# Copying three inputs inside DRAM first, so that the blocks of a VectorE transpose are read and written in order

## The chip, the cores and the metric

The kernel runs on one core of one Trainium2 chip. The metric is the device time of one execution in microseconds, the median of several runs. TensorE (PE in the profile) multiplies matrices, VectorE (DVE) and ScalarE (ACT) work on elements, GpSimd (POOL) helps, and SyncE (SP) issues every DMA of this kernel on one queue.

## What is computed

The reference is a gated linear attention followed by a feed-forward block with the hardswish activation, all in float32.

```
batch, n_heads, seq, head_dim = (4, 8, 768, 48)
for t in range(S):
    state = alpha[:, :, t, :, None] * state + np.einsum('bhd,bhe->bhde', k[:, :, t], v[:, :, t])
    y[:, :, t] = np.einsum('bhd,bhde->bhe', q[:, :, t], state)
x = y.transpose(0, 2, 1, 3).reshape(B * S, H * D)       # 3072 x 384
h = x @ w_in                                            # 384 x 2048
g = h * np.clip(h + 3.0, 0.0, 6.0) / 6.0
out = g @ w_out                                         # 2048 x 384
```

## The kernel before

**Chunks.** The 4 x 768 tokens are cut into 24 chunks of 128 tokens, numbered j = 0 to 23. For a chunk, alpha, k and q are wanted with the feature on the partition (head pair p in 0 to 3; two heads of a pair at partitions 0 and 64) and the token along the free axis. Decay products along the tokens are scans on VectorE (`decay`, L309; `growth`, L320); k and q are scaled by them (`scaled`, L332); scores, masking, the state's update and the output are small matmuls with VectorE and ScalarE work between (`scores` L346, `masked` L356, `update` L429, `attend` L455). Two chunks make a group g; its 256 tokens go through the feed-forward block. From group 2 on, both large products are done by fast matrix multiplication, with sums made on VectorE (L537 to L541, L647, L664) and products on TensorE (`product1`, L600; `product`, L703).

**How a chunk arrives.** `load_akq` (L248) loads alpha, k or q of one chunk. Chunks 0 to 5 are turned on TensorE. From chunk 6 on, a load fills a tile of `quads` (two buffers per name, by j modulo 2, L237) with four DMAs, one per group of 32 partitions (L262): partition u of a group holds tokens 4u to 4u+3, each with its 48 features, so that every run in DRAM is four tokens long (768 bytes, or 640 where the first 32 features are skipped). `by_blocks` (L285) then turns all of it on VectorE in one instruction, 32 x 32 words at a time; since token 4u+v lies at place v of partition u, the output goes to every fourth word ("(u v)" read as "v u"). It serves alpha (`place_alpha`), k and q (`transposed`).

**k by token.** `update` also needs k with the token on the partition. From chunk 8 on, `turn_k` (L388) transposes it back in blocks on VectorE into the k tile of `quads`, `write_k` (L393) writes that to a DRAM tile called far with four DMAs (L396), and `read_k` (L400) reads it back as kb with four more (L404). All wait on the same SP queue as the loads, the loads of v (L272) and the stores of the output (L724).

**The order.** Nothing is scheduled by the compiler: the body ends with one list of words (L751 to L900), and each engine runs its instructions in the order of that list. "la", "lk", "lq" load alpha, k, q; "ca", "tk", "tq" turn them; "kt", "kw", "kr" are the three steps of the exchange through far; "u" the update; "lv" loads v; "O" stores. An engine that waits holds up everything behind it on its own queue only.

The loads and the turn, as they stand:

```
        t = src.rearrange("(p a) (u v) d -> a u p (v d)", a=2, v=V)
        for o in range(4):
            skip = BLK * (o % 2)
            nc.sync.dma_start(out=to[BLK * o : BLK * (o + 1), :, 0 : V * D - skip],
                              in_=t[o // 2, :, :, skip : V * D])
...
        nc.vector.transpose(out=to.rearrange("r p (u v) -> r p v u", v=V),
                            in_=quads[name, j % NQ][:, :, :, 0:BLK])
```

Of the kernel before, what the change touches and what calls it, by code (L numbers as in the profile page):

```python
# [8 lines left out]
FP = mybir.dt.float32  # L9
# [8 lines left out]
def kernel(  # L18
# [32 lines left out]
    nc = tc.nc  # L51
    B, H, S, D = q.shape
# [195 lines left out]
    def load_akq(name, j):  # L248
        src = rows({"a": alpha, "k": k, "q": q}[name], j)
        if j < FIRST:  # L250
            nc.sync.dma_start(out=ring[name, j % NR][:, :, 0:D],
                              in_=src.rearrange("h s d -> s h d"))
            return
        to = quads[name, j % NQ]
        if j < FIRST + NQ:
            for o in (BLK, 3 * BLK):
                nc.gpsimd.memset(to[o : o + BLK, :, V - 1, D - BLK : BLK], 1.0)
        to = to.rearrange("r p v d -> r p (v d)")
        t = src.rearrange("(p a) (u v) d -> a u p (v d)", a=2, v=V)
        for o in range(4):  # L260
            skip = BLK * (o % 2)
            nc.sync.dma_start(out=to[BLK * o : BLK * (o + 1), :, 0 : V * D - skip],  # L262
                              in_=t[o // 2, :, :, skip : V * D])

# [20 lines left out]
    def by_blocks(to, name, j):  # L285
        nc.vector.transpose(out=to.rearrange("r p (u v) -> r p v u", v=V),
                            in_=quads[name, j % NQ][:, :, :, 0:BLK])
# [433 lines left out]
    def store2(g, i):  # L721
# [8 lines left out]
        "lq": lambda j: load_akq("q", j), "lv": load_v, "w": load_weight,  # L730
# [19 lines left out]
    with tc.manual_schedule():  # L750
# [3 lines left out]
               dx.0 w.2 d2.2 kb.1.0 ck.1 lq.1 r.2 sm.0.1 st.1 tq.1.2 q.1 d3.2 z.0.3 d1.2 dx.2 lv.1.1  # L754
               u.1.3.1 sv.1.0 sm.1.0 p.2 sm.1.1 sc.1.0.2 m.1 ya.0.3 yb.0 cy.0 lq.2 w.1 d1.1 tq.2.1
               q.2 d4.2 lk.2 tk.2.3 k.2 fa.2.0 d4.0 st.2 sc.2.0.2 d2.1 d3.1 m.2 dx.1 d4.1 qa.1.1
               lk.3 la.3 ta.3.1 ca.3 la.4 fa.0.1 sv.1.1 w.3 r.3 ta.4.3 ca.4 r.4 tk.3.1 k.3 kb.2.0
               qa.1.0 d2.3 ya.1.2 yb.1 cy.1 fa.1.2 lq.3 ck.2 d1.3 p.3 d3.3 lv.2.2 u.2.3.2 sm.2.0
               d4.3 fb.2 tq.3.1 q.3 fb.1 qa.2.0 sm.2.1 sv.2.0 st.3 fr.0.2.0 fg.0.2 lk.4 tk.4.0
               sv.2.1 w.5 d2.5 k.4 d3.5 d1.5 qa.3.0 d4.5 qa.2.1 sc.3.1.3 m.3 w.6 d2.6 d1.6 d3.6 d4.6  # L760
               lv.3.0 lq.4 w.7 kb.3.2 fb.0 f.0.3.3 kb.4.0 ya.2.1 ck.3 u.3.3.2 sm.3.0 fr.0.3.1 fg.0.3
               fr.0.1.0 fg.0.1 qa.3.1 sv.3.0 sm.3.1 p.4 d2.7 sv.3.1 d1.7 d3.7 d4.7 f.0.5.0 fr.0.5.1
               fr.0.0.0 fg.0.5 fg.0.0 tq.4.3 ck.4 la.5 ta.5.2 f.0.6.3 ca.5 w.4 d2.4 ya.3.0 yb.3 cy.3
               fr.0.6.1 yb.2 cy.2 w.9 d2.9 q.4 qa.4.1 d1.4 d1.9 dx.4 la.6 w.8 d3.4 r.5 lk.5 w.10
               d3.9 p.5 ca.6 fg.0.6 d4.9 w.12 lq.5 lv.4.1 d2.8 d3.8 f.0.7.2 d1.8 st.4 d4.8 d4.4 w.11
               fr.0.7.0 fg.0.7 f.1.7.0 fr.1.7.1 fg.1.7 sc.4.0.2 m.4 f.1.1.1 fr.1.1.0 fg.1.1 f.1.3.3
               fr.1.3.1 d2.10 d1.10 tk.5.3 f.1.0.2 d2.12 d3.10 d4.10 w.13 fg.1.3 fr.1.0.0 fg.1.0 k.5
               d3.12 lq.6 f.1.6.0 f.1.2.1 u.4.1.0 sm.4.0 d1.12 d4.12 sv.4.0 qa.4.0 ya.4.2 fr.1.6.1
               fg.1.6 w.15 tq.5.3 fa.4.3 sv.4.1 d2.11 kb.5.1 d2.13 fr.1.2.0 f.1.4.2 fr.1.4.1 d1.11
               sm.4.1 q.5 r.6 d3.11 d3.13 fg.1.4 d4.11 lv.5.0 lk.6 tq.6 p.6 d2.15 d3.15 fg.1.2 d1.13  # L770
               d4.13 sc.5.0.3 yb.4 f.1.5.0 fr.1.5.1 fg.1.5 tk.6 m.5 b.1.0.2 fb.4 b.1.1 d1.15 d4.15
               st.5 y.5 w.14 la.7 lk.7 cy.4 d2.14 qa.5.1 ck.5 b.0.0.1 fr.0.4.0 d3.14 k.6 q.6 ca.7
               fg.0.4 d1.14 d4.14 x.0 y.1 y.10 b.0.1 y.0 y.2 u.5.2 P.1.0.0 K.1.0 qa.5.0 sv.5.0
               qa.6.1 P.1.1.3 b.0.2 b.1.2 kb.6.0 ya.5.3 y.6 s.1.0.0 sm.5.0 sv.5.1 G.1.0.0 tk.7
               s.1.1.1 s.1.2.3 x.1 yb.5 cy.5 b.1.3 sc.6.1.2 lv.6.2 ck.6 u.6.3.0 s.1.3.2 x.2 P.1.2
               b.0.3 K.1.1 y.7 s.1.4 s.1.5 y.11 y.3 r.7 xc.2.1 x.3 y.4 y.8 xc.2.3 k.7 xc.2.0 xc.2.4
               y.9 y.12 y.16 y.13 y.15 P.1.3.3 K.1.2 P.1.4 bo.1 P.1.5 xc.2.5 G.1.1.1 P.1.6 y.14 y.17
               y.19 xc.2.6 sm.6.0 G.1.2.2 y.20 M.2.0.2 lv.12.1 la.8 O.1.1 O.1.0 ca.8 y.18 y.21 y.23
               so.1 G.1.3.3 n.2.0.8 bo.0 lq.7 lv.7.0 O.1.2 m.6 xc.2.2 xc.2.10 xc.2.7 tq.7 r.8 p.7
               xc.2.8 sv.6.1 M.2.15.3 M.2.1 kb.7.3 n.2.1.9 M.2.16 M.2.2 n.2.2.10 M.2.7.0 n.2.7.11  # L780
               sm.6.1 xc.2.9 q.7 p.8 M.2.3 M.2.4 n.2.4.12 M.2.8 o.2.0.0 M.2.5 n.2.5.13 qa.7.0 sv.6.0
               st.7 lk.8 O.1.3 lq.8 lk.9 la.9 la.10 tk.8 tq.8 lq.10 lq.9 ya.6.1 yb.6 M.2.9 z.1.3
               M.2.18.1 o.2.1.0 e.2.1.1 M.2.10 cy.6 ck.7 sc.7.0.2 u.7.1.3 n.2.10.14 M.2.11 qa.7.1
               ca.9 la.11 y.22 M.2.6.2 h.2.1 q.8 m.7 e.2.0.0 h.2.0 n.2.11.15 qa.6.0 n.2.18.10 qa.8.1
               M.2.12 M.2.19 n.2.12.12 M.2.13 sm.7.0 sv.7.1 r.9 k.8 o.2.3.0 sv.7.0 ya.7.0 y.24
               o.2.5.0 n.2.13.12 o.2.2.0 yb.7 cy.7 sc.8.1.2 xc.3.1 o.2.2.1 e.2.2.1 xc.3.3 o.2.3.1
               M.2.14 xc.3.4 xc.3.0 xc.3.5 o.2.4.0 xc.3.7 xc.3.6 o.2.6.0 P.2.0.1 M.3.0.2 M.2.17
               h.2.2 o.2.6.1 e.2.3.0 h.2.3 o.2.7.0 K.2.0 n.3.0.12 M.3.1 n.3.1.9 e.2.5.1 M.3.7.0
               n.3.7.13 xc.3.8 o.2.7.1 xc.3.2 kt.8 e.2.6.0 h.2.6 tk.9 M.3.2 n.3.2.10 e.2.4.0 P.2.1.3
               h.2.4 h.2.5 s.2.0.14 e.2.7.0 G.2.0.1 h.2.7 M.3.3 M.3.4 n.3.4.8 k.9 s.2.1.11 M.3.8  # L790
               o.3.0.0 ca.10 kt.9 P.2.3.3 s.2.2.15 s.2.3.14 lv.8.2 kw.8 kr.8 lk.10 sm.7.1 xc.3.9
               M.3.5 n.3.5.11 K.2.2 e.3.0.1 xc.3.10 M.3.9 o.3.1.0 P.2.2 K.2.1 u.8.0.3 M.3.18.2 s.2.5
               M.3.10 n.3.10.14 n.3.18.15 e.3.1.0 s.2.4 P.2.4 tq.9 h.3.0 st.8 sv.8.0 M.3.11 n.3.11.8
               tk.10 p.9 sm.8.0 q.9 r.10 k.10 qa.9.0 qa.9.1 m.8 sm.8.1 h.3.1 M.3.19 o.3.5.0 kt.10
               P.2.5 G.2.2.0 st.9 M.3.12 sc.9.0.1 qa.8.0 n.3.12.10 o.3.3.0 kw.9 lv.9.0 kr.9 sv.8.1
               u.9.2.3 sm.9.0 sv.9.1 sv.9.0 G.2.1.2 sm.9.1 st.10 M.3.15.2 M.3.16 M.3.6.3 M.3.13 m.9
               o.3.4.0 o.3.6.0 tq.10 n.3.13.10 o.3.2.0 e.3.4.1 ya.8.2 yb.8 ya.9.3 yb.9 cy.9 M.3.14
               M.3.17 cy.8 xc.4.1 P.2.6 e.3.5.0 G.2.3.3 o.3.2.1 xc.4.3 h.3.4 xc.4.4 o.3.6.1 xc.4.5
               xc.4.0 xc.4.6 e.3.2.1 M.4.0.0 n.4.0.10 P.3.0.1 xc.4.7 o.3.7.0 p.10 h.3.5 o.3.3.1
               xc.4.8 M.4.7.3 M.4.1 xc.4.2 h.3.2 o.3.7.1 lk.11 O.2.2 tk.11 e.3.6.0 e.3.3.1 h.3.3  # L800
               P.3.1.2 e.3.7.1 n.4.1.13 M.4.2 K.3.0 ca.11 q.10 h.3.6 r.11 k.11 h.3.7 n.4.7.15
               lv.10.2 lv.11.0 kw.10 sc.10.0.1 kr.10 G.3.0.0 u.10.3.2 sm.10.0 qa.10.1 n.4.2.14 M.4.3
               M.4.4 M.4.8 s.3.0.9 xc.4.9 s.3.2.12 s.3.1.11 P.3.3.2 n.4.4.8 M.4.5 o.4.0.0 e.4.0.0
               sv.10.1 sm.10.1 xc.4.10 kt.11 O.2.0 O.2.3 lq.11 m.10 s.3.3.9 s.3.5 M.4.9 o.4.1.0
               P.3.2 sv.10.0 st.11 n.4.5.11 K.3.2 la.13 M.4.18.0 p.11 tq.11 lk.12 tk.12 K.3.1 M.4.10
               n.4.10.9 q.11 qa.10.0 n.4.18.12 e.4.1.1 la.12 s.3.4 ca.12 h.4.0 r.12 P.3.5 G.3.2.1
               h.4.1 M.4.11 P.3.4 n.4.11.8 M.4.12 n.4.12.14 qa.11.0 M.4.19 p.12 G.3.1.3 lq.12 kw.11
               O.2.1 tq.12 kr.11 u.11.3 sc.11.0.2 sv.11.0 O.3.1 lk.13 P.3.6 qa.11.1 M.4.6.2 G.3.3.2
               k.12 o.4.3.0 m.11 sm.11.0 sv.11.1 kt.12 M.4.13 n.4.13.14 q.12 o.4.3.1 e.4.3.0 o.4.2.0
               o.4.6.0 h.4.3 o.4.2.1 ya.10.1 ya.11.0 yb.10 yb.11 cy.11 cy.10 xc.5.1 ca.13 xc.5.3  # L810
               M.4.15.1 M.4.16 M.4.14 P.4.0.2 o.4.4.0 M.4.17 xc.5.4 o.4.5.0 xc.5.0 xc.5.5 M.5.0.0
               o.4.6.1 e.4.2.1 h.4.2 P.4.1.3 qa.12.1 e.4.4.0 xc.5.6 o.4.7.0 h.4.4 o.4.7.1 tk.13
               K.4.0 n.5.0.14 M.5.1 e.4.7.1 h.4.7 e.4.5.0 xc.5.2 h.4.5 xc.5.7 G.4.0.3 e.4.6.1 h.4.6
# [119 lines left out]
```

## Time and profile before

| | us |
|---|---|
| median of 3 runs (lowest, highest) | 535.48 (535.39, 535.66) |
| span of the profiled execution, first to last instruction | 533.7 |
| TensorE busy in it | 524.6 |
| VectorE busy in it | 477.2 |
| ScalarE busy in it | 257.2 |
| share of the 16 DMA engines taken by the one queue | 42.5% |

The profile records one execution. The span leaves out what lies before the first and after the last instruction; against the median that is 1.8 us. Matmuls are pipelined and their ends are modelled, so a busy TensorE is not by itself a TensorE at its peak; the waits say more. The granted TensorE clock is 1.00 throughout.

### The profile page before, as it was taken

Reading aid. Unit: us, or ns where it says so; the run is one execution under the profiler, and the core shown is the slowest. Engines: PE = TensorE matmul, PEld = TensorE weight load, DVE = VectorE, ACT = ScalarE, POOL = GpSimd, SP = SyncE. Lnnn points to the kernel's source line nnn. Section 1 sums busy time; section 2 is a strip of 40 time slices with the busy share of each in tenths; the row PEclk is TensorE's granted clock in tenths of the full one; section 3 lists DMA queues with packets and bytes.
Section 4 is the critical chain, followed back from the end, with each engine's and each line's share of the span. In section 5 each row is a group of like instructions: output and inputs, shape, how many; then the busy total and the mean of one; then the engine's idle time right before and its main releaser. Section 6 shows DMA issues by size and latency. Waiting matters only on the chain.

```text
span 533.7 us, 15143 instructions
## 1 busy us (share of the span) xinstructions
PE 524.6 (98%) x6306; PEld 499.4 (94%) x6306; DVE 477.2 (89%) x849; ACT 257.2 (48%) x503; POOL 50.4 (9%) x71
## 2 busy tenths in 40 slices
PE   8799999999999999999999999999999999999997
PEld 7698886789999999999999999999999999999997
DVE  6999989999999999998999999999999899496382
ACT  3889865212653553553544444642634544553340
POOL 5333425100000000000000000000000000000000
DMA  9998876005615155254344355044454042100001
GB/s 174 217 252 256 215 216 152 21 2 154 152 30 116 32 121 135 57 140 95 87 110 113 91 124 140 19 120 102 115 136 104 11 110 43 44 2 2 15 16 37
DMA packets 124100, 54.40 MB, mean 102 GB/s; under 512 B 83328, under 2 KB 116864, under 8 KB 124032
## 3 DMA queue, kind: packets, MB, share of 16 engines
q1 hardware_dynamic: 124032, 53.44, 42.5%
q8 instruction: 49, 0.80, 0.6%
q14 instruction: 19, 0.16, 0.1%
HBM read 44.50 MB, written 8.91 MB: 100 GB/s over the span
## 4 chain that ended last, share of the span: by engine, by line
PE 85%; DVE 8%; POOL 2%; DMA 2%; ACT 1%; issue 1%; SPq 1%; DVEq 0%; POOLq 0%
PE m_ps L703 34%; PE m_ps L600 34%; PE m_ps L478 5%; PE t_ps L455 4%; PE t_ps L346 2%; PE t_ps L429 2%; PE m_ps L489 2%; PE t_ps L282 1%; DVE rings L647 1%; DMA v<-in_v_dram 1%; DVE raw L537 1%; ACT raw L191 1%; DMA kq<-in_k_dram 1%; DVE g_sb L647 1%; DVE w L537 1%
## 5 line engine op out<-in xcount | busy, mean ns | idle before, releaser
L606 ACT COPY g_sb<-m_ps 128x512 f32<-128x512 f32 x110 | 63.6, 584 | 124.9 <-PE m_ps L600 104.1
L703 PE MATMUL m_ps<-w,g_sb 128*128 128x192 f32 x704 | 121.7, 327 | 0.0
L703 PEld LDWEIGHTS m_ps<-w,g_sb 128*128 128x128 f32 x704 | 113.7, 190 | 0.4
L703 PE MATMUL m_ps<-rings,g_sb 128*128 128x192 f32 x528 | 91.5, 326 | 0.0
L703 PEld LDWEIGHTS m_ps<-rings,g_sb 128*128 128x128 f32 x528 | 85.4, 190 | 0.1
L600 PE MATMUL m_ps<-xc,w 128*128 128x128 f32 x640 | 82.7, 277 | 0.3 <-DVE w L541 0.3
L600 PEld LDWEIGHTS m_ps<-xc,w 128*128 128x128 f32 x640 | 77.5, 192 | 1.5 <-issue 0.5
L494 ACT ACTIVATE r<-g_sb,half 128x512 f32<-128x512 f32 x80 | 56.8, 722 | 32.9 <-DVE g_sb L541 12.1
L498 DVE SCALAR_TENSOR_TENSOR g_sb<-r,g_sb 128x512 f32<-128x512 f32 x80 | 53.6, 682 | 4.6 <-ACT r L494 4.2
L600 PE MATMUL m_ps<-xT,raw 128*128 128x128 f32 x400 | 52.5, 277 | 0.0
L600 PEld LDWEIGHTS m_ps<-xT,raw 128*128 128x128 f32 x400 | 48.6, 192 | 0.6
L409 POOL TENSOR_TENSOR st<-sm,R 128x192 f32<-128x192 f32 x20 | 12.9, 643 | 353.8 <-DVE sm L439 306.7
L647 DVE TENSOR_TENSOR g_sb<-g_sb 128x512 f32<-128x512 f32 (+1 forms) x55 | 42.0, 795 | 0.2
L600 PE MATMUL m_ps<-xT,w 128*128 128x128 f32 x320 | 42.0, 276 | 0.0
L600 PEld LDWEIGHTS m_ps<-xT,w 128*128 128x128 f32 x320 | 39.3, 192 | 0.1
L366 ACT COPY A<-q 48x256 f32<-48x256 f32 x88 | 35.5, 404 | 5.0 <-DVE q L332 3.7
L356 DVE TENSOR_TENSOR A<-t_ps,mask 64x256 f32<-64x256 f32 x96 | 36.0, 414 | 0.4
L478 PE MATMUL m_ps<-xT,w 128*128 128x256 f32 x144 | 32.8, 382 | 0.0
L600 PE MATMUL m_ps<-xc,raw 128*128 128x128 f32 x240 | 31.8, 276 | 0.0
L309 DVE TENSOR_TENSOR_SCAN R<-t,ones 128x516 f32<-128x516 f32 x24 | 29.7, 1236 | 1.1 <-ACT t L300 1.0
L478 PEld LDWEIGHTS m_ps<-xT,w 128*128 128x128 f32 x144 | 26.7, 190 | 3.6
L600 PEld LDWEIGHTS m_ps<-xc,raw 128*128 128x128 f32 x240 | 29.6, 192 | 0.1
(104 smaller groups left out, 731.0 us busy)
## 6 DMA issues: line engine op xcount, KB each, us to landing
raw<-in_moe_w_out_dram SPq DMA_DIRECT2D x8, 768.0 KB, 5.2
raw<-in_moe_w_in_dram SPq DMA_DIRECT2D x6, 768.0 KB, 6.8
v<-in_v_dram SPq DMA_DIRECT2D x48, 96.0 KB, 3.0
out_dram<-oh SPq DMA_DIRECT2D x44, 96.0 KB, 1.7
far<-kq SPq DMA_DIRECT2D x64, 64.0 KB, 2.2
kb<-far SPq DMA_DIRECT2D x64, 64.0 KB, 2.0
aq<-in_alpha_dram SPq DMA_DIRECT2D x36, 96.0 KB, 2.5
qq<-in_q_dram SPq DMA_DIRECT2D x36, 96.0 KB, 2.4
```

The source lines that it names most:

```text
L309: nc.vector.tensor_tensor_scan(out=reverse(R, n - 1, n), data0=reverse(ax, n, n), data1=reverse(ones, n, n), initial=0.0, op0=ALU.mult, op ...
L356: nc.vector.tensor_tensor(out=to[:, a], in0=sc[a][half], in1=mask[half, half].unsqueeze(1).to_broadcast([HB, NP, HB]), op=ALU.mult)
L366: nc.scalar.copy(out=to[:, a], in_=Q_t[j][64 * a : 64 * a + D, :, half])
L409: nc.gpsimd.tensor_tensor(out=st, in0=sm, in1=R_t[j][:, :, 0:1].to_broadcast([C, NP, D]), op=ALU.mult)
L455: nc.tensor.matmul(y_of(j, (i + 1) // 2, p)[:, HB * b : HB * b + HB], vb[:, p, e : e + 32], A_t[j][:, b, 2 * p + a], start=(b == 0 and i = ...
L478: nc.tensor.matmul(h[:, f], w1[:, kk, o : o + C], xT_t[g][:, kk], start=(kk == 0), stop=(kk == KT - 1))
L494: nc.scalar.activation(out=to, in_=h, func=AF.Relu, bias=half, scale=1.0 / 6.0)
L498: nc.vector.scalar_tensor_tensor(out=to, in0=r, scalar=1.0, in1=h, op0=ALU.min, op1=ALU.mult)
L600: nc.tensor.matmul(acc[g][i][:, f * C : (f + 1) * C], spots[w][:, f * C : (f + 1) * C], x_of(g, x), start=(first and f == 0), stop=last, s ...
L606: nc.scalar.copy(out=slots[z], in_=acc[g][i])
L647: nc.vector.tensor_tensor(out=out, in0=in0, in1=in1, op=ALU.subtract)
L703: nc.tensor.matmul(to[g], a, rhs[:, f], start=(first and f == 0), stop=(last and f == HF - 1), skip_group_check=True)
```

## The change

For chunks 10 to 23 (`MOVED = 10`), a new step `move` ("mv" in the list) copies alpha, k and q of the chunk from the inputs to DRAM tiles ma, mk and mq, which have two buffers each: one DMA per name, eight runs of 6144 words, head order (pair, a) turned into (a, pair). `load_moved` then fills the tile of `quads` from the copy, in another layout: partition u of a group of 32 holds token 32v+u at place v, so that one run is the 32 features (or the last 16) of one token, 128 or 64 bytes; four DMAs per load as before, each with 512 runs. The pads behind the 16 features, which the long runs used to fill with other data, are set once per buffer on GpSimd. `by_blocks` reads the tile and writes its output in order.

```
+        if j >= MOVED:
+            load_moved(name, j)
+            return
...
+    def in_blocks(name, j):
+        t = quads[name, j % NQ].rearrange("r p v d -> r (p v d)")[:, 0 : NP * C]
+        return t.rearrange("r (p v d) -> r p v d", p=NP, v=V)
+
+    def move(j):
+        for name, t in (("a", alpha), ("k", k), ("q", q)):
+            to = moved_t[name, j] = far.tile([2, NP, C * D], FP, tag="m" + name, name="m" + name)
+            nc.sync.dma_start(out=to, in_=rows(t, j).rearrange("(p a) s d -> a p (s d)", a=2))
+
+    def load_moved(name, j):
+        to = in_blocks(name, j)
+        if j < MOVED + NQ:
+            for o in (BLK, 3 * BLK):
+                nc.gpsimd.memset(to[o : o + BLK, :, :, D - BLK : BLK], 1.0 if name == "a" else 0.0)
+        to = to.rearrange("r p v d -> r (p v) d")
+        t = moved_t.pop((name, j)).rearrange("a p (v u d) -> a u (p v) d", u=BLK, v=V)
+        for o in range(4):
+            skip = BLK * (o % 2)
+            n = min(BLK, D - skip)
+            nc.sync.dma_start(out=to[BLK * o : BLK * (o + 1), :, 0:n],
+                              in_=t[o // 2, :, :, skip : skip + n])
...
     def by_blocks(to, name, j):
+        if j >= MOVED:
+            nc.vector.transpose(out=to.rearrange("r p (v u) -> r p v u", v=V),
+                                in_=in_blocks(name, j))
+            return
```

In the list of words only the fourteen "mv" are new; every other word keeps its place. mv.10 and mv.11 stand ahead of la.8. Each later mv.j stands right behind the last load of chunk j-2, whose copies' buffers it takes over:

```
... lv.12.1 mv.10 mv.11 la.8 O.1.1 O.1.0 ca.8 ...
... lv.8.2 kw.8 kr.8 lk.10 mv.12 ... kw.9 lv.9.0 kr.9 ...
... lq.11 mv.13 ... la.13 ... lk.12 ... lq.12 mv.14 kw.11 ... kr.11 ...
... kr.12 la.14 ... lk.14 lq.13 mv.15 O.3.0 O.3.3 lv.13.2 kw.13 O.4.0 lq.14 mv.16 ... lq.15 ...
... lk.20 mv.22 ... kw.19 kr.19 ... lk.21 mv.23 kw.20 ...
```

## The prediction

> **What bounds the kernel now.** I read the page's busy row first, then the chain that ended last, then who waited for whom on TensorE from 110 us on, then the VectorE groups with shapes kept apart, and last the DMA queue: its issues in order of time, and its packets in single windows. The columns of the busy row are busy time, share of the span and instructions; the next row is the chain's share by engine; the last is TensorE's only wait after 110 us (total, times, longest).
>
> ```profile
> PE 524.6 (98%) x6306; PEld 499.4 (94%) x6306; DVE 477.2 (89%) x849; ACT 257.2 (48%) x503; POOL 50.4 (9%) x71
> PE 85%; DVE 8%; POOL 2%; DMA 2%; ACT 1%; issue 1%; SPq 1%; DVEq 0%; POOLq 0%
> PE m_ps L600 <- DVE w L541: 0.3, 1, 0.3
> ```
>
> TensorE carries the end. In the chain, VectorE stands only before 128.04 us; from there to 530.8 us every piece is a matmul, and the one wait is 0.3 us, at 128 us. VectorE is busy 89%, but nobody on TensorE waits for it later. The first operation that the change touches on VectorE is the alpha transpose of chunk 10, at 163.2 us. So whatever VectorE saves there has at most tenths of a us to give.
>
> The two kinds of transpose that matter (line, shapes, count | busy, mean ns | idle before):
>
> ```profile
> L286 DVE STREAM_TRANSPOSE q<-qq 128x512 f32<-128x512 f32 x18 | 20.2, 1121 | 0.0
> L286 DVE STREAM_TRANSPOSE t<-aq 128x512 f32<-128x512 f32 x18 | 20.1, 1115 | 0.0
> L391 DVE STREAM_TRANSPOSE kq<-k 128x512 f32<-128x512 f32 x16 | 11.2, 697 | 0.0
> ```
>
> L286 writes every fourth word, L391 writes runs of 32 words; same size, 1.12 against 0.70 us.
>
> Now the queue that the change loads. The first three rows are SP's issues around chunk 9 (start, time, line, transfer, count); the fourth is the matmuls of that chunk's state update on TensorE.
>
> ```profile
> 163.28 2.23 SPq L262 DMA_DIRECT2D kq<-in_k_dram  x4
> 165.61 2.57 SPq L396 DMA_DIRECT2D far<-kq  x4
> 169.85 1.82 SPq L404 DMA_DIRECT2D kb<-far  x4
> 179.72 0.82 PE L429 MATMUL t_ps<-v,kb 64*64 64x48 f32 x32
> ```
>
> Every chunk from 8 on sends its k through DRAM (far, then kb) on this one queue, and `update` needs kb. The last of the four kb reads is issued three quarters into its row and lands 2.0 us later (the page's median): 173.2 us for chunk 9, 6.5 us ahead of its use at 179.72. The same difference for chunks 9 to 23 is 6.5, 3.5, 4.8, 6.9, 4.5, 6.5, 4.0, 5.9, 9.3, 4.7, 4.2, 5.8, 12.9, 3.3 and 6.7 us, median 5.8. That is all the cover that this exchange has.
>
> Last, what packets cost, in four windows that hold nearly one kind each (packets, MB, share of 16 engines):
>
> ```profile
> q1 hardware_dynamic: 205, 0.63, 46.6%
> q1 hardware_dynamic: 3102, 1.94, 62.5%
> q1 hardware_dynamic: 1161, 0.25, 30.0%
> q1 hardware_dynamic: 1584, 0.20, 41.2%
> ```
>
> 68 to 72 us holds 3 KB packets of w_out: 46.6% of 4 us times 16 engines, over 205, is 145 ns each. 133.3 to 146 holds the present loads (768 and 640 bytes): 40.9 ns. 146 to 150 is mostly v (192 bytes): 16.5 ns. 157 to 160 is the far write (128 bytes): 12.5 ns.
>
> **The change, part by part.** *Transposes.* 42 of them (alpha, k, q of chunks 10 to 23) now write in runs as L391 does: 42 x (1.12 - 0.70) = 17.6 us less on VectorE; the bounds are 0, if the order of the words doesn't matter, and these 17.6. On the path: 0. The only wait that it could shorten is the 0.3 us above, and that lies before them.
>
> *Pads.* Twelve memsets of 32 partitions on GpSimd, at the loads of chunks 10 and 11. They wait for the buffers of chunks 8 and 9; GpSimd is idle for 31.5 us before its work at 166.65 us. 0.
>
> *Loads.* Each has 4 x 512 pieces of 128 or 64 bytes in place of 4 x 128 long ones. Issuing 512 pieces takes SP 0.65 us (far: 2.57 for four), a present load's 0.465: 0.74 us more per load. On the engines 2048 x 16.5 ns / 16 = 2.1 us replaces 512 x 40.9 / 16 = 1.3 us; bounds 1.6 us (12.5 ns) and 5.2 us (40.9 ns). I take 16.5, the nearest row: short pieces from DRAM to SBUF. With room on the queue the extra is hidden; behind the copies it adds the 0.74 us once to each hold-up below.
>
> *Copies.* Three per chunk, DRAM to DRAM, 196,608 bytes each, as eight runs of 24,576. How many of the 16 engines share one, the trace doesn't show: every transfer before has 32, 64 or 128 outermost steps. It shows that runs aren't cut (2,112 packets between 156.7 and 161.0 us, where one far exchange issues four times 512 runs), so at most eight engines can work on eight runs. The source's outermost step counts only 2 (the two heads of a pair, a=2, then four pairs), the destination's 8. Bounds: eight engines with one run each, or two with four runs each. By the w_out row a run is 8 x 145 ns = 1.16 us: 1.2 us a copy on eight, 4.65 us on two. I take two, because whole outermost steps are what both sides can hand out without cutting either; both ends stay in play. [...]
>
> The speed itself has bounds too. The share reads 138.0% between 9 and 14 us, so packets on an engine overlap up to 1.4 deep, and a copy may take 4.65 / 1.38 = 3.4 us. Nothing in the trace reads and writes DRAM at once; if that halves the speed, it is 9.3 us. I take 4.65, the row with the longest packets.
>
> *What is queued behind them.* SP's order is otherwise the same. Each copy set stands right behind the last load of chunk j-2, whose landing it waits for (2.4 us by the page's medians, mostly beside the first copy's own drain). In most places the next transfers are the far/kb exchange of an earlier chunk: after the copies of 12 come far and kb of 9, after 14 those of 11, after 15 of 13, after 17 of 14, after 22 of 19. Those need all 16 engines, the two busy ones also, and come after the three copies there: 3 x 4.65 = 14.0 us. With 0.7 us for a load, less the 5.8 us of cover, TensorE stands still 14.0 + 0.7 - 5.8 = 8.9 us, 12 times (chunks 12 to 23): 107 us. The copies of 10 and 11 go out near 91 us, where SP otherwise waits until 121.67; six of them drain in 28 us, by 119, and the alpha load of chunk 8 behind them lands near 121, ahead of its transpose at 124.83. 0, with 3 us to spare.
>
> *Sum.* The profiled span is 533.7 us; the median of the runs is 535.5, so 1.8 us lie around it. 533.7 + 107 + 1.8 = 642 us.
>
> A cross-check by load alone: per chunk the two engines carry 14.0 (copies) + 6.3 (three loads) + 1.1 (v) + 1.6 (far) + 0.8 (kb, eight packets of 2 KB each at two thirds of 145 ns) + 0.7 (two output stores) = 24.5 us, where TensorE takes 19.7 us per chunk ((464.16 - 168.73) / 15). Even with perfect overlap 14 x 4.8 = 67 us are missing, which would be 603 us.
>
> **Rivals.** *Hidden copies (not slower).* If a copy runs on eight engines, three hold the queue for 3.5 us, under the 5.8 us of cover; then nothing reaches TensorE, VectorE's 17.6 us are off the path, and the time stays 535.5. It decides where a copy takes less than about 1.8 us. For it: the eight runs, and SP's long idle stretches (127 us waiting for outputs alone). Against: the outermost 2, and the least covers of 3.3 and 3.5 us, which such a hold-up could still graze.
>
> *Half speed.* Copies at 9.3 us: 27.9 + 0.7 - 5.8 = 22.8 us, 12 times, 274 us, and 809 us. For it: both ends in DRAM. Against: far's writes into DRAM cost 12.5 ns a packet, less than v's reads from it.
>
> *Small packets dear.* If the 64- and 128-byte reads cost 40.9 ns each, loads take 5.2 us in place of 2.1, 9.3 us more per chunk: 24.5 + 9.3 - 19.7 = 14.1 us, 14 times: 197 us, and 733 us. For it: present loads cost 40.9 ns; against: v's 192-byte pieces cost 16.5.
>
> **How the numbers follow.** A measurement can tell about 0.2%, or 1.1 us, from no change. The forecast, two engines at 3.4 to 7.2 us a copy: 0.80. Hidden copies: 0.11, of which 0.08 within 0.2%, 0.02 faster and 0.01 slower by a grazed cover. Half speed: 0.05; dear packets: 0.04. Faster 0.02, same 0.08, slower 0.90. The range goes from the copy at 3.4 us (12 x (10.2 + 0.7 - 5.8) = 61 us, 597; some covers are longer, so 588) to one at 7.2 us (12 x 16.5 = 198, 734) and the dear packets' 733; up to 740. It leaves out hidden copies, half speed, and little more.
>
> **What would show it.** Right: TensorE's waits led by L429, the update, on the kb transfer; far and kb landing over 10 us after issue where they follow copies; copies landing one after another some 4 to 5 us apart; the transposes at 0.70 us; VectorE's idle time growing by far more than it saves. Wrong: copies landing within 3 us of issue and TensorE still without waits, or TensorE waiting for something other than a transfer behind a copy.

## The result, and the profile after

| | before | after |
|---|---|---|
| median of the runs, us (lowest, highest) | 535.57 (535.39, 535.73) | 631.64 (631.19, 634.57) |
| span of the profiled execution | 533.7 | 629.5 |
| TensorE busy in it | 524.6 | 544.3 |
| VectorE busy in it | 477.2 | 464.0 |
| mean granted TensorE clock | 1.00 | 0.932 |

The changed kernel is slower: ratio 1.181, 95% interval 1.178 to 1.183. The forecast was 642, range 588 to 740.

Lines are shifted by the change: the far write is L428, the kb read L436, the update L461, the copies L278, the moved loads L290. First the busy row and the chain's shares of the page, then TensorE's waits from 110 us on (total, times, longest):

```profile
PE 544.3 (86%) x6306; PEld 517.3 (82%) x6306; DVE 464.0 (74%) x849; ACT 257.6 (41%) x503; POOL 54.1 (9%) x83
PE 50%; DVE 16%; SPq 16%; DMA 12%; issue 2%; POOL 1%; ACT 1%; DVEq 0%; POOLq 0%
PE t_ps L461 <- DMA kb<-far: 56.9, 10, 14.9
PE t_ps L461 <- DMA v<-in_v_dram: 15.5, 1, 15.5
PE m_ps L735 <- DVE g_sb L679: 2.9, 1, 2.9
```

One wait of 0.3 us has become 76 us of waits, nearly all at the update, on transfers. With the 19.7 us that TensorE is busy longer, they make up the 95.8 us by which the span grew. TensorE's share of the chain falls from 85% to 50%, and SP's own sequencer holds 16% where it held 1%.

Each moved transpose got as short as was reckoned (moved layout, then the old one, which chunks 6 to 9 keep):

```profile
L315 DVE STREAM_TRANSPOSE k<-kq 128x512 f32<-128x512 f32 x14 | 9.9, 706 | 5.2 <-DMA kq<-mk 5.2
L318 DVE STREAM_TRANSPOSE k<-kq 128x512 f32<-128x512 f32 x4 | 4.4, 1110 | 0.0
```

Now the same place as before, the exchange of chunk 9. SP's issues in order of time (start, time, line, transfer, count), and then the first matmuls of the update on TensorE, with their wait in brackets:

```profile
166.90 0.66 SPq L278 DMA_DIRECT2D ma<-in_alpha_dram  x1
167.60 0.64 SPq L278 DMA_DIRECT2D mk<-in_k_dram  x1
168.28 0.60 SPq L278 DMA_DIRECT2D mq<-in_q_dram  x1
168.98 9.39 SPq L428 DMA_DIRECT2D far<-kq  x4
...
182.35 1.72 SPq L436 DMA_DIRECT2D kb<-far  x4
```

```profile
184.89 0.42 PE L461 MATMUL t_ps<-v,kb 64*64 64x48 f32 x2 [5.05 <-DMA kb<-far]
```

Three copies go out in 1.9 us. The far write behind them takes SP 9.39 us to issue in place of 2.57: SP doesn't merely see it land late, it is held in the issue itself. kb then leaves 12.5 us later than before (182.35 against 169.85), the cover was 6.5 us, and TensorE waits 5.05 us.

How fast a copy is shows where nothing else runs, in the stretch after the first six copies (110 to 114 us; 40 slices of 0.1 us, GB/s in each; then packets, MB, share of 16 engines):

```profile
GB/s 0 0 0 0 0 0 246 0 246 0 0 0 0 0 0 246 0 246 0 0 0 0 0 0 246 0 246 0 0 0 0 0 0 246 0 0 246 0 0 0
q1 hardware_dynamic: 10, 0.20, 11.4%
```

Each 246 is one packet of 24,576 bytes. They end in pairs, one pair every 0.9 us, and the share is that of two engines (2 of 16 is 12.5%): each of two engines moves a run in 0.91 us, 27 GB/s, and a copy of eight runs takes 3.65 us. Two engines is what the forecast took from the source's outermost step of 2; the trace now agrees. The 3.65 us are nearer to its lower bound, 3.4 us from overlapping packets (4.65 / 1.38), than to the 4.65 us taken from the w_out row.

### The profile page after: what moved, and what is told of

The parts are those of the page before. It is cut to its first block, busy times and chain, and to the rows that moved or that the text cites. A ratio compares the mean times of both kernels' runs of the same rounds, so it can differ in the third digit from the quotient of the medians.

```text
span 629.5 us, 15199 instructions
## 1 busy us (share of the span) xinstructions
PE 544.3 (86%) x6306; PEld 517.3 (82%) x6306; DVE 464.0 (74%) x849; ACT 257.6 (41%) x503; POOL 54.1 (9%) x83
## 4 chain that ended last, share of the span: by engine, by line
PE 50%; DVE 16%; SPq 16%; DMA 12%; issue 2%; POOL 1%; ACT 1%; DVEq 0%; POOLq 0%
PE m_ps L632 17%; PE m_ps L735 17%; SPq L428 6%; DMA far<-kq 6%; SPq L290 5%; PE m_ps L510 5%; PE t_ps L487 3%; PE t_ps L461 2%; DMA mq<-in_q_dram 2%; DMA kb<-far 2%; PE m_ps L521 2%; DVE g_sb L679 2%; SPq L436 2%; DVE g_sb L530 2%; DMA v<-in_v_dram 1%
## 5 line engine op out<-in xcount | busy, mean ns | idle before, releaser
L735 PE MATMUL m_ps<-w,g_sb 128*128 128x192 f32 x704 | 123.6, 330 | 0.0
L735 PEld LDWEIGHTS m_ps<-w,g_sb 128*128 128x128 f32 x704 | 115.7, 193 | 0.5
L735 PE MATMUL m_ps<-rings,g_sb 128*128 128x192 f32 x528 | 95.3, 336 | 2.9 <-DVE g_sb L679 2.9
L735 PEld LDWEIGHTS m_ps<-rings,g_sb 128*128 128x128 f32 x528 | 89.0, 197 | 3.3 <-DVE g_sb L679 3.1
L632 PE MATMUL m_ps<-xc,w 128*128 128x128 f32 x640 | 85.8, 284 | 0.3 <-DVE w L573 0.3
L461 PE MATMUL t_ps<-v,kb 64*64 64x48 f32 x704 | 21.4, 244 | 74.5 <-DMA kb<-far 56.9
L461 PEld LDWEIGHTS t_ps<-v,kb 64*64 64x64 f32 x704 | 18.0, 156 | 78.4 <-issue 62.4
L632 PEld LDWEIGHTS m_ps<-xc,w 128*128 128x128 f32 x640 | 80.7, 198 | 1.5 <-issue 0.4
L530 DVE SCALAR_TENSOR_TENSOR g_sb<-r,g_sb 128x512 f32<-128x512 f32 x80 | 53.6, 683 | 13.4 <-ACT r L526 13.2
L632 PE MATMUL m_ps<-xT,raw 128*128 128x128 f32 x400 | 56.2, 290 | 0.0
L632 PEld LDWEIGHTS m_ps<-xT,raw 128*128 128x128 f32 x400 | 52.2, 204 | 0.7
L441 POOL TENSOR_TENSOR st<-sm,R 128x192 f32<-128x192 f32 x20 | 12.9, 644 | 419.9 <-DVE sm L471 365.0
L471 DVE TENSOR_TENSOR s<-t_ps,st 128x192 f32<-128x192 f32 x20 | 7.0, 352 | 56.7 <-PE t_ps L461 37.7
L632 PE MATMUL m_ps<-xT,w 128*128 128x128 f32 x320 | 42.9, 280 | 0.0
L632 PEld LDWEIGHTS m_ps<-xT,w 128*128 128x128 f32 x320 | 40.1, 195 | 0.1
L632 PE MATMUL m_ps<-xc,raw 128*128 128x128 f32 x240 | 31.8, 276 | 0.0
```

What stands on the lines that cost most here:

```text
L461: nc.tensor.matmul(ps_t["u", j, b][64 * a : 64 * a + 64, p], kb_t[j][half, p, 64 * a : 64 * a + 64], v_t[j][half, b, 2 * p + a, 0:D], star ...
L530: nc.vector.scalar_tensor_tensor(out=to, in0=r, scalar=1.0, in1=h, op0=ALU.min, op1=ALU.mult)
L632: nc.tensor.matmul(acc[g][i][:, f * C : (f + 1) * C], spots[w][:, f * C : (f + 1) * C], x_of(g, x), start=(first and f == 0), stop=last, s ...
L735: nc.tensor.matmul(to[g], a, rhs[:, f], start=(first and f == 0), stop=(last and f == HF - 1), skip_group_check=True)
```

## The experiments

Each was run with the kernel before on the same chip, whose medians were 535.49 to 535.65 us. All intervals are 95%.

**1. The copies alone.** Loads and transposes stay as they were before; the copies are made and nobody reads them.

```
-        if j >= MOVED:
-            load_moved(name, j)
-            return
```

(and the same in `by_blocks`)

> Only the copies of the changed kernel, three per chunk in the same places, and nobody reads them: loads from the inputs in long runs and transposes as before the change. Theory (the copies alone make the hold-ups): TensorE still waits 50 to 80 us for kb and v, and the time is 600 to 632 us. Rival A (short pieces): without them the time is 535 to 545. Rival B (waits for landings between copies and loads): those links are gone here too, so the time falls below 570.

Measured: 620.17 us (619.46 to 621.42), ratio 1.158 (1.157 to 1.160). TensorE's waits:

```profile
PE t_ps L454 <- DMA kb<-far: 47.8, 10, 12.3
PE t_ps L454 <- DMA v<-in_v_dram: 13.6, 1, 13.6
```

The copies by themselves, read by no one, cost 84.7 of the 96.1 us, with the same two waits. The loads with their short pieces add 11.5.

**2. The transposes alone.** Only the order of the words written by the transposes of chunks 10 to 23 is changed, with the loads of before; the tokens of those chunks then stand in another order.

```
-        nc.vector.transpose(out=to.rearrange("r p (u v) -> r p v u", v=V),
-                            in_=quads[name, j % NQ][:, :, :, 0:BLK])
+        to = to.rearrange("r p (v u) -> r p v u" if j >= 10 else "r p (u v) -> r p v u", v=V)
+        nc.vector.transpose(out=to, in_=quads[name, j % NQ][:, :, :, 0:BLK])
```

> The kernel before with one edit: the transposes of chunks 10 to 23 write in runs. The loads are unchanged, so tokens come out in another order; the order is what is left out. Theory: VectorE's busy time falls by about 17 us (42 transposes from 1.12 to 0.70 us), TensorE has no waits to shorten, and the time stays within 0.2% of before, 534.5 to 536.5 us. Rival (VectorE's pace sets TensorE's somewhere that the waits don't show): 525 to 533 us.

Measured: 535.48 us, ratio 1.000 (0.9991 to 1.0009). The busy row against that of before:

```profile
PE 524.4 (98%) x6306; PEld 499.4 (94%) x6306; DVE 463.5 (87%) x849; ACT 257.2 (48%) x503; POOL 50.4 (9%) x71
```

VectorE works 13.7 us less and nobody gains. The whole aim of the change is worth nothing here. That it is 13.7 us and not the 17.6 of 42 shorter records comes from overlap: the next instruction used to start 0.96 us after such a transpose (median) and now starts 0.63 us after it, and 42 x 0.33 = 13.9 us.

**3. More outermost steps per copy.** The copy is cut by head parity into two DMAs, first with four outermost steps (four runs of 24,576 bytes each), then with sixteen (1,536 bytes each).

```
+            src = rows(t, j).rearrange("(p a) (g s) d -> a g p (s d)", a=2, g=16)
+            for a in range(2):
+                nc.sync.dma_start(out=to[a].rearrange("p (g x) -> g p x", g=16), in_=src[a])
```

> The changed kernel with each copy cut in two (one per parity) of four runs of 24,576 bytes, so that four engines share it. Theory: six runs of 0.91 us on each of four engines, 5.5 us a set in place of 10.9; against a median cover of 5.8 us less 0.7 for a load, hold-ups of 0 to 3 us remain at the chunks with the least cover: waits of 2 to 12 us, 537 to 550 us, and clock losses small. Rival A (short pieces): above 575 us. Rival C (the bytes written to and read from DRAM, however spread): as the changed kernel, 620 to 632 us.

> The changed kernel with each copy cut in two transfers (one per parity of the head) of 16 outermost steps of 1,536 bytes, so that 16 engines can share it; loads, transposes and places in the list as in the changed kernel. Theory (two engines hold up the exchange): a set of copies keeps an engine busy for about 0.6 us per name in place of 3.65, TensorE's waits after 128 us fall from 76 us to under 2, the granted clock stays at 1.00, and the time is 535 to 537 us. Rival A (the short pieces of the loads jam the queue): they are all still here, so the waits stay above 30 us and the time above 575. Rival B (SP is held by the landings that the copies wait for and by twice as many copy issues, six of 0.6 us): waits of 10 to 40 us remain, 550 to 580 us.

Measured: four steps 564.12 us, ratio 1.054 (1.052 to 1.055); sixteen steps 549.36 us, ratio 1.027 (1.025 to 1.030). Both are above what the theory allowed, and the second is nearly at its rival B (549.4 us against 550, waits of 9 us against 10), which the next experiment takes up. But the order is as it should be, if a copy runs on as many engines as it has outermost steps. That was the author's assumption; these runs show the times alone: two steps 631.6 us, four 564.1, sixteen 549.4. With sixteen the page gives a copy half 2.4 us to landing, and the waits are small:

```profile
PE t_ps L463 <- DMA kb<-far: 6.2, 5, 2.2
PE t_ps L463 <- DMA v<-in_v_dram: 3.0, 1, 3.0
```

The bytes are the same; 82 of 96 us went with more outermost steps, 67.5 of them already with four, where the runs are as long as before. 13.9 us are left, which "copies on all engines are free" doesn't explain.

**4. Another issuer.** First the sixteen-step copies, then the copies of the change itself, issued by GpSimd on its own queue; nothing else is changed.

```
-                nc.sync.dma_start(
+                nc.gpsimd.dma_start(
```

> As the kernel with copies on sixteen engines (split by head parity, six DMAs per chunk, 549.4 us), but the copies are issued by GpSimd on a queue of its own, at the same places in the list. Theory (what is left of the loss there, 14 us, is SP's time for 84 more issues and its waiting for the buffers of the copies, with far and kb behind them): TensorE's waits shrink from 11.5 us to under 4, and the time is 536 to 540 us. Rival (the moved loads with their 2,048 short pieces, or the traffic of the copies, are what is left): 545 to 552 us. Rival (GpSimd's own work, the state's update, waits behind the copies, or the copies wait behind it): over 555 us, with new waits of TensorE on GpSimd or on loads.

> The changed kernel with its copies as they are (one DMA of eight runs, two engines), issued by GpSimd on its own queue. Theory (SP is held while it issues far behind the copies, 9.4 us for four issues in place of 2.6, and far and kb stand behind the copies in one queue): with two queues the packets of far and kb take turns with the copies' on the two engines, SP is free, and what is left is those engines' load: 11 us of copies plus 10.5 us of other packets per chunk against 19.7 us of TensorE, 14 x 1.8 = 25 us, so about 545 to 570 us. Rival (the two engines finish the copies' 24,576-byte packets first whatever queue they come from, and every transfer waits for its last packet there): 600 us or more. Rival (two queues hide it all): under 540 us.

Measured: sixteen steps 536.22 us, ratio 1.0010 (1.0002 to 1.0019); eight runs 554.63 us, ratio 1.035 (1.033 to 1.037). TensorE's waits, of the first and of the second kernel, and the far write of chunk 9 in the second:

```profile
PE t_ps L463 <- DMA v<-in_v_dram: 0.3, 1, 0.3
PE m_ps L634 <- DVE w L575: 0.2, 1, 0.2
```

```profile
PE t_ps L461 <- DMA kb<-far: 6.2, 2, 5.6
PE t_ps L461 <- DMA v<-in_v_dram: 5.6, 1, 5.6
```

```profile
168.89 4.39 SPq L428 DMA_DIRECT2D far<-kq  x4
```

The first removes the remaining 13.9 us down to 0.6: the moved loads and the traffic, which this kernel still has, are harmless, and what was left of the loss came with the copies' place on SP's queue (84 issues more, and what stood behind them).

The second is the surprise: the change's copies, on another queue, cost 19 us in place of 96. The range of its theory is met, but not by its mechanism, two engines shared by two queues. The runs are still whole: both pages count 404 packets of 8 KB or more, the copies' 336 among them (the rest of GpSimd's 3,360 packets are under 512 bytes). But the copies ran on more engines at once. The first six move 148 GB/s from 96 to 100 us and take 50.6% of the time of the 16 engines, with nothing else on them; on SP's queue it was 49 GB/s and 11.4%. They also leave at other times, since GpSimd doesn't stand in SP's line (the set ahead of chunk 9's far write at 163.50 us in place of 166.90). So how much of the 77 us is the queue and how much the engines stays open.

In the first kernel the change of issuer was worth 13 us; the 77 us of the second don't measure it, since the engines changed too.

**5. Doses.** The kernel before, with 1, 2, 3, 4 and 6 unread copies put right ahead of the far write of five chunks.

```
+    def copies(j, n):
+        for i in range(n):
+            to = far.tile([2, NP, C * D], FP, tag=f"m{i}", name=f"m{i}")
+            nc.sync.dma_start(out=to, in_=rows((alpha, k, q)[i % 3], j).rearrange(
+                "(p a) s d -> a p (s d)", a=2))
```

> The kernel before, with copies that nobody reads (one DMA of eight runs of 24,576 bytes each, as in the change) put right before the far write of five chunks: 1 copy before that of chunk 10, 2 before 13, 3 before 15, 4 before 18, 6 before 20. All loads, layouts and transposes are those of before. Theory (a copy holds the queue for 3.65 us, two engines at 912 ns per packet, and a wait is the sum of the copies less the cover): covers of 3.5, 4.5, 4.0, 4.7 and 5.8 us give waits of TensorE at the five updates of about 0 to 1, 2.8, 7, 9.9 and 16 us, in all 36 us, and some 2 us more of busy time behind each wait of over about 4 us, where the granted clock falls. Rival (4.65 us a copy, as first forecast): 1.2, 4.8, 10, 13.9 and 22 us. Rival (copies cost nothing by themselves, the hold-up comes from the moved loads): no waits, 535.5 us.

Measured, in a single run: 571.22 us. The waits behind 3, 4 and 6 copies, and SP's issue of the far write behind the six:

```profile
306.41 0.42 PE L435 MATMUL t_ps<-v,kb 64*64 64x48 f32 x2 [3.78 <-DMA kb<-far]
374.47 0.42 PE L435 MATMUL t_ps<-v,kb 64*64 64x48 f32 x2 [7.13 <-DMA kb<-far]
433.47 0.45 PE L435 MATMUL t_ps<-v,kb 64*64 64x48 f32 x2 [14.20 <-DMA kb<-far]
```

```profile
407.74 18.65 SPq L402 DMA_DIRECT2D far<-kq  x4
```

The wait grows with the number of copies, by 3.35 us from three to four and by 7.07 from four to six. As they stand that is 3.4 to 3.5 us a copy; but the exchanges differ in cover, and with 4.0, 4.7 and 5.8 us added back it is 4.1. So the doses show that a copy costs some 3.4 to 4.1 us, and the 3.65 rests on the window above. Two copies cost nothing and one 1.2 us (chunk 11's update is that much later than before); from two copies on, the waits are 1.8 to 3.2 us below the theory's. After each of the three waits the next update slips by another 2.8 to 3.2 us without waiting for anything; TensorE's busy time is 7.3 us longer in all (531.9 against 524.6).

**6. Keeping TensorE busy while it waits.** That second slip pointed to the clock. In the changed kernel, the windows at the first hold-up (time, then busy time and count of PE, PEld, DVE, ACT, POOL, the granted clock, the DMA share, GB/s):

```profile
184.00:190.00 6.00, 4.62 (x47) 4.43 (x48) 2.31 (x7) 1.40 (x4) 0.88 (x3) 0.50 0.43 79
...
192.00:196.00 4.00, 4.00 (x147) 3.79 (x146) 1.84 (x4) 2.79 (x5) 0.00 (x0) 1.00 0.26 44
```

From 184 to 190 us, with the wait ending at 184.89, the clock is 0.50, and sixteen matmuls of L632 take 3.78 us where they normally take 2.05. The half clock begins at 183.9 us, 4.1 us into this pause, and ends at 190.7, 5.8 us after it. But in the same kernel a pause of only 2.9 us, from 224.0 to 226.9 us, is also followed by half clock, from 228.3 to 231.7, so the 4 us in the expectations of experiments 5 and 6 is no limit. How long a pause must be was not shown. The forecast had left all this out. The experiment puts small matmuls, unused, ahead of seven updates:

```
+    def warm(i, n):
+        for _ in range(n):
+            nc.tensor.matmul(banks[i][:, 0:C], ident, ident, start=True, stop=True)
```

> The changed kernel, with small extra matmuls (128x128, result unused, some 0.22 us each) on TensorE right before the updates of seven chunks: 18 of them at 9, 44 at 11, 56 at 13, 24 at 15, 62 at 17, 62 at 19, 10 at 20, about as long as TensorE stood still there. Theory (the 19.7 us of extra busy time are the half clock that follows a pause of more than some 4 us): the mean granted clock goes from 0.93 back to 0.99 or more, the waits stay about as they are less the time that the extra matmuls fill, and the time falls by 10 to 17 us, to about 615 to 621 us. Rival (the transfers set the pace, so that whatever the clock gives is waited for again): the granted clock goes up, the time stays within 2 us of 631.6. Rival (the extra matmuls only add work): over 633 us.

Measured: 628.75 us (624.61 to 633.36), ratio 1.174 (1.172 to 1.176). The busy row, and the row of the extra matmuls:

```profile
PE 602.2 (95%) x6858; PEld 574.9 (91%) x6858; DVE 464.1 (73%) x849; ACT 257.4 (41%) x503; POOL 54.0 (9%) x83
```

```profile
L568 PE MATMUL t_ps<-ident 128*128 128x128 f32 x552 | 63.3, 276 | 0.0
```

The mean granted clock rose to 0.978, but that mean counts the filled pauses. The kernel's own work took 602.2 - 63.3 = 538.9 us: 5.4 us of the 19.7 were won in the profiled execution, which is the slowest of the five; the median is 2.9 us lower than without them, within the spread of the runs. So the expected 10 to 17 us didn't come; the experiment removed too little of the clock loss to say what all of it is worth. The trace of the changed kernel itself says what it costs: in windows of half a us, added up, TensorE is busy for 38.0 us at half clock. If work takes twice as long there, as the sixteen matmuls nearly do, 19.0 of the 19.7 us are the clock. The same count for experiment 5 gives 7.3 of its 7.3 us.

**7. Another order on the same queue.** If the exchange suffers because it stands right behind the copies, it should help to put the copies behind the exchange. First each set behind the next kb read (first pair of lines); then, with four buffers per name, the set of chunk j behind the kb read of chunk j-3 (the last line, against the first).

```
- ... mv.12 ... kr.9 ... kr.10 ... lq.11 mv.13 la.13 ... lq.12 mv.14 kw.11 ... kr.11 ...
+ ... kr.9 mv.12 ... kr.10 ... lq.11 ... lq.12 kw.11 ... kr.11 mv.14 mv.13 la.13 ...
+ ... kr.9 mv.12 ... kr.10 mv.13 ... lq.11 la.13 ... lq.12 kw.11 ... kr.11 mv.14 ...
```

> The changed kernel with the same transfers, and from chunk 12 on each chunk's copies (with a load of the same chunk that stood between, for chunks 13, 15 and 19) put right behind the next kb read on SP's queue, not ahead of the far write. Theory (the loss is what is queued behind the copies, the exchange of an earlier chunk): the exchange is no longer held, and the loss falls to less than half, 555 to 585 us; what is left is loads that land late behind copies. Rival (the load of the two engines as such sets the pace): 600 us or more, with the waits moved to other transfers.

> The changed kernel with the same copies (one DMA of eight runs each, two engines, SP's queue), four buffers for each of ma, mk and mq in place of two, and from chunk 12 on the copies of chunk j put right behind the kb read of chunk j-3, so that no far write of the same chunk stands behind them and the loads of the copied chunk come about one exchange later; two alpha loads (17 and 18) stand a little later so that they don't wait for their own copies. Theory (the price of a copy is paid by what is queued right behind it): TensorE's waits on kb nearly vanish, SP is held by loads that have time, and what is left is the load of the two engines, 11 + 10.5 us per chunk against 19.7: about 25 us, 550 to 570 us. Rival (one queue for all: whatever stands behind the copies is late, and something always does): 590 us or more. For the kernel with the copies behind the exchange but in pairs out of order (615 us), where loads waited for six copies at once, the same theory had been 555 to 585 us.

Measured: 615.19 us, ratio 1.148 (1.147 to 1.150), and 603.06 us, ratio 1.127 (1.123 to 1.131). The first was badly built: where two sets fell behind the same kb read, the later chunk's came first, so that a load waited for six copies. SP's last copy issue there and the load behind it, 21.1 us later:

```profile
267.47 0.60 SPq L278 DMA_DIRECT2D mq<-in_q_dram  x1
289.18 1.91 SPq L290 DMA_DIRECT2D qq<-mq  x4
```

The second has no such pair, and still loses 67.5 us. Its wait on kb is all but gone, and others have come; the load behind a set is held as the far write was (8.84 us for four issues, normally 2.0):

```profile
PE m_ps L735 <- DVE g_sb L679: 12.5, 2, 9.7
PE t_ps L461 <- issue: 10.3, 1, 10.3
...
PE t_ps L461 <- DMA kb<-far: 1.7, 2, 1.5
```

```profile
227.05 8.84 SPq L290 DMA_DIRECT2D kq<-mk  x4
```

VectorE waits 45 us for moved loads here, where it was 5.2 us in the changed kernel. The theory missed and the rival held: in every order tried, something stood behind the copies and was held, whatever it was.

**8. Where VectorE seemed to set the pace.** Before 128 us the chain runs through VectorE. Two kernels move only early loads (sixteen-step copies on SP): chunks 6 and 7 and alpha of 8, with the copies ahead of the loads; then five loads whose transposes stand before 128 us, with the copies where SP is idle.

```
+    EARLY = {("q", 6), ("k", 6), ("a", 7), ("k", 7), ("a", 8)}
```

> The moved layout where VectorE's transposes stand on the path: copies (split by head parity, 16 outermost steps, 16 engines) and moved loads for chunks 6 and 7 and for alpha of chunk 8 alone; all later chunks as before. If VectorE's time from 76 to 128 us sets the end there, five to seven transposes of 0.42 us less give 2 to 3 us: 532.5 to 533.5 us. Rival (the copies and the longer issues on the one queue delay the weight and chunk loads of the beginning): 536 to 542 us.

> The moved layout for five loads only whose transposes stand before 128 us, where VectorE sets the pace: q and k of chunk 6, alpha and k of chunk 7, alpha of chunk 8. The copies run on sixteen engines (two DMAs of sixteen outermost steps each) and are issued where SP stands idle before, so that no weight load waits for them: behind the v load of chunk 4, behind the q load of chunk 6, behind the last weight load, and ahead of the alpha load of chunk 8. Theory: 5 x 0.42 = 2.1 us less, 533.4 us (532.9 to 534.2). Rival (the copies still delay a load, or VectorE waits there for something else): 535.3 us or more.

Measured: 536.91 us, ratio 1.0026 (1.0016 to 1.0036), and 535.22 us, ratio 0.9993 (0.9984 to 1.0002). In the first, six copy issues and the k load ahead of them put the last weight load off from 81.27 to 87.66 us, and VectorE waits 3.05 us for that weight. In the second, VectorE is ahead by 1.15 us at the fourth transpose, and then waits for TensorE:

```profile
120.82 0.36 DVE L753 TENSOR_TENSOR oh<-m_ps,p 128x192 f32<-128x192 f32 x1 [0.94 <-PE m_ps L737]
...
124.35 0.70 DVE L317 STREAM_TRANSPOSE t<-aq 128x512 f32<-128x512 f32 x1
```

Before, this last transpose began at 124.83. Of 2.1 us, 0.5 arrive: TensorE was as full as VectorE there, and its matmuls at 115 to 125 us stand at the same times to 0.06 us. No kernel here beats the one before by more than can be measured.

## Why the prediction was right, and where it was wrong

**Transposes, pads, first copies: right.** 0.70 us each; worth nothing on the path (experiment 2). Only VectorE's saving was smaller, 13.2 us in place of 17.6, since neighbouring instructions overlap. The first six copies drain by about 115 us, the alpha load of chunk 8 is in time, and TensorE's first fast product starts at 127.98 us, before it was 128.04.

**Two engines: right**, shown by the pairs in the window and its share of 11.4%, where two of 16 engines are 12.5%; the times of experiment 3 fit it. **A copy at 4.65 us: too long.** It takes 3.65; the w_out packets of 3 KB, from which 4.65 was worked out, move 21 GB/s (145 ns each), one run of 24,576 bytes 27 (0.91 us).

**Twelve hold-ups of 8.9 us each: the step that failed.** The lag of an update is its start in the trace after less that in the trace before. The table has what each chunk adds to it and how long TensorE waited, against the number of copy sets that the list puts ahead of the end of its exchange since the last one:

| chunk | sets | cover before, us | sets x 10.95 - cover | lag added, us | waits, us |
|---|---|---|---|---|---|
| 9 | 1 | 6.5 | 4.5 | 5.2 | 5.5 |
| 11 | 2 | 4.8 | 17.1 | 16.3 | 14.3 |
| 13 | 2 | 4.5 | 17.4 | 13.8 | 14.2 |
| 14 | 1 | 6.5 | 4.5 | 3.9 | 0 |
| 15 | 1 | 4.0 | 7.0 | 6.5 | 6.9 |
| 17 | 2 | 9.3 | 12.6 | 15.7 | 15.5 |
| 19 | 2 | 4.2 | 17.7 | 15.1 | 15.5 |
| 20 | 1 | 5.8 | 5.2 | 6.3 | 3.9 |
| sum | 12 | 45.6 | 85.8 | 82.8 | 75.8 |
| 10, 12, 16, 18, 21 | 0 | | 0 | 12.9 together | 0 |

(10.95 is 3 x 3.65; the 14.3 at chunk 11 have the 2.9 us of L735 in them.) Twelve sets meet eight exchanges, four of them two at a time, and seven of the eight made TensorE wait; at chunk 14, which lagged by the clock after the wait before it, the exchange was in time. A cover can be spent once per exchange, not once per set, so the forecast subtracted it four times too often. Counted rightly, with 4.65 us a copy, it would have been 4 x 8.9 + 4 x (2 x 14.7 - 5.8) = 130 us, and 665.5; with 3.65 us a copy and twelve covers, 12 x 5.85 = 70 us, and 606. Of these two errors one takes away 23 us and the other adds 37; with both mended, the table's 85.8 us give 621, and the clock, which was left out, adds nearly 20. That 642 lies so near to 631.6 is luck.

**Left out: the clock.** The five chunks with no set before them, and chunk 14, add 16.8 us without a wait, 1.9 to 3.9 each. That is what experiment 5 shows behind each of its waits (2.8 to 3.2 us), and TensorE's busy time is 19.7 us longer at the same instruction count. Of these, 19.0 are accounted for by the work at half clock (experiment 6).

**Left out: SP held in the issue.** The forecast let far and kb queue on the engines. The traces show SP itself held (9.39 us for the far write of chunk 9 in place of 2.57), so that what stands behind slips (kb by 12.5 us), and in experiment 7 the better of two other orders wins only 29 of the 96 us. What in the queue holds SP was not shown.

**Loads: 0.74 us more per load was too much.** Far's 512 pieces, from which it was taken, need 0.65 us per issue; the 512 pieces of a moved load need 0.49 at the median, and four of them 2.02 in place of 1.86: 0.16 us. With the copies on SP, the loads and transposes together add 11.5 us; with the copies elsewhere they cost nothing (experiment 4).

**The cross-check by load** gave 67 us with 14.0 us of copies per chunk; with 10.95 it is 14 x (21.5 - 19.7) = 25 us, far under the 96 measured. On SP's queue order and holding count, not load. The 19 us on GpSimd's queue don't test it, since those copies ran on more than two engines.

**The rivals.** Copies were nearly hidden only with sixteen outermost steps and another queue, 536 us; with sixteen and SP's queue it was 549. Half speed and dear packets are ruled out by the window and by experiment 4.

## What to carry to other kernels

Before pricing a DMA, look at the outermost step of both sides: here eight runs of 24,576 bytes, with an outermost step of 2 in the source, sat on two engines (11.4% of the time of the 16), and behind three such copies on the same queue SP took 9.39 us to issue a far write in place of 2.57. Count the cover of a stalled exchange once for each exchange, not once for each thing put ahead of it, and look which sets fall into the same gap. Look at the granted clock behind a pause of TensorE: here each stretch at half clock cost 1.7 to 3.5 us. Before shortening an instruction on a busy engine, look for a wait that names that engine: here VectorE, busy 89%, worked 13.7 us less and the time stayed at 535.48 us; trying the short form alone shows that in one run.

## What the runs showed of the hardware that was not expected

An SP issue of four small writes took 9.39 us behind three copies (chunk 9) and 18.65 behind six (experiment 5), in place of 2.6. The same copies on GpSimd's queue cost 19 us rather than 96; there they ran on more than two engines at once (148 GB/s in place of 49), so the share of the queue itself stays open. A pause of 5 us on TensorE was followed by 5.8 us at half clock, and one of 2.9 us by 3.4. Each of the eight stretches at half clock in the changed kernel lasts 3.4 us or two, three or five times as long (6.8, 10.2, 17.1).
